# One core, sliding-window attention and expert layers: moving the loads of q, k and v to other places in the queues

## The chip, the cores and the metric

The kernel runs on 1 core of one Trainium2 chip. The metric is the device time of one execution in microseconds (us). Before the change, three runs took 228.25, 230.02 and 230.86; the median is 230.02.

## The reference

For 8 batches, 8 heads, 576 positions and 64 elements a head, each query attends to itself and the 63 positions before it. The result of a batch, 576 x 512, is averaged over its positions; the average picks one of 8 experts, and the batch goes through that expert's two matrices.

```python
scores = scale * np.matmul(q, k.transpose(0, 1, 3, 2))
mask = (rel >= 0) & (rel < window)             # rel = query - key, window = 64
attn = softmax(np.where(mask, scores, -1e9))   # exp, divided by its sum
x = np.matmul(attn, v)                         # heads side by side: B, S, 512
...
logits = x.mean(axis=1) @ w_gate               # 512 -> 8
e_idx = np.argmax(logits, axis=1)
gate_w = softmax(logits)[e_idx]
out = gate_w * (np.maximum(x @ w1[e_idx], 0) @ w2[e_idx])   # 512 -> 1024 -> 512
```

All inputs are float32 in device memory.

## The kernel before

**Units, steps and batches.** The work is cut into 16 units, each half a batch (four heads): unit u belongs to batch u // 2. For a unit, `transpose_qk` turns q and k (TensorE) and ScalarE or VectorE copies them out of PSUM; `scores(u, c)` for c = 0, 1, 2 multiplies q and k, takes the exponential (ScalarE, L389) and, from unit 2 on, multiplies the result tile `pt` with a 0/1 mask (VectorE, L391); `values(u, s)` multiplies `pt` with v (L413) and VectorE divides by the row sums (L427, L429). `cast_part` and `cast_v` make the float16 copies of v that `values` reads (VectorE, L303); `cast_v(u)` does all three parts of a unit. `transpose_x` (L450, L458) prepares the batch's attention result for the expert layers and adds up the gate's input (L476, L480).

**The gate and the experts.** `gate(b)` computes the logits, finds the expert (VectorE, L492 to L500) and loads its number into a register of GpSimd; `load_w1(b)` and `load_w2(b)` then fetch that expert's matrices, 2 MB each in float32, cast to float16 on the way. `expert_up` (L557, eight pieces a batch) and `expert_down` (L571, L580, five pieces) are handed out in small portions by `experts(amount)` between the pieces of attention, so that TensorE always has something to do. The program order written here is the order in which each engine works; each engine takes its instructions strictly in that order.

**The order of the work.** Units 0 to 3 are written out by hand ahead of the loop (L686 to L758); L760 is the loop over steps t = 4 to 19, where step t does the attention of unit t, the transposes of unit t + 1 and expert pieces of earlier batches. `next_gate` (L764) runs gate b = t // 2 - 1 in every even step, so the weights of batch b are fetched in step 2b + 2 and first used in step 2b + 3.

**The loads.** Three kinds of loads matter here.
- `load_qk(u)` (L207) puts two DMAs into GpSimd's queue, q (L211) and k (L214) of one unit, cast to bfloat16. It needs nothing but a free tile; there are six of each.
- `load_w1` and `load_w2` (L534, L539; for batch 0 in two halves, L531) are in GpSimd's queue too, and wait for the gate.
- `load_v(b)` (L220) is a DMA in SyncE's queue (L227), float32, one for a whole batch, three tiles. Ahead of it GpSimd writes one column of the tile; SyncE's DMA waits for that write. Without a second argument the write is a memset (L223), which waits for nothing and holds the DMA only until GpSimd comes to it. With the argument `behind` it is a copy of one column of that tile (L226), so the load starts only when that tile is written.

The output tiles go out through SyncE's queue as well (L575, L588), so output and v stand in one line, in program order.

Before the change the places are these. Ahead of the loop: `load_qk(3)` and `load_qk(4)` after the transposes of unit 1; then gate 0, w1 and w2 of batch 0, `load_qk(5)`, v of batch 2 behind the first half of batch 0's w1, `load_qk(6)`, v of batch 3. In step 4, after gate 1: w1, w2, v of batch 4, `load_qk(7)`. At the head of step 5: `load_qk(8)` and `load_qk(9)`. From then on an even step t has, behind its gate, w1, `load_qk(t + 4)` (up to t = 10), w2, and v of batch t // 2 + 2; an odd step has `load_qk(t + 4)` at its head. q and k are four units ahead.

Of the kernel before, what the change touches and what calls it, by code (L numbers as in the profile page):

```python
# [156 lines left out]
def kernel(  # L157
# [11 lines left out]
    B, H, S, D = q.shape  # L169
# [5 lines left out]
    NU = 2 * B  # L175
# [4 lines left out]
    def P(ins):  # L180
        tc.keep_in_program_order(ins)
        return ins
# [25 lines left out]
    def load_qk(u):  # L208
        qn = qkn.tile([128, 2, NT * D], BF16, tag="qn")
        kn = qkn.tile([128, 2, NT * D], BF16, tag="kn")  # L210
        P(nc.gpsimd.dma_start(out=qn, in_=qv[u]))  # L211
        if u == 0:
            load_v(0)
        P(nc.gpsimd.dma_start(out=kn, in_=kv[u]))  # L214
        qk_tiles[u] = (qn, kn)
# [3 lines left out]
    def load_v(b, behind=None):  # L219
        vn = vpool.tile([128, NM, D], FP32, tag="vn")  # L220
        if behind is None:

            P(nc.gpsimd.memset(vn[:, 0, 0:1], 0.0))  # L223
        else:

            P(nc.gpsimd.tensor_copy(out=vn[:, 0, 0:1], in_=behind))  # L226
        P(nc.sync.dma_start(out=vn, in_=vv[b]))  # L227
        v_tiles[b] = vn
# [70 lines left out]
    def copy_on(eng, out, in_):  # L299
        if eng is nc.scalar:  # L300
            P(nc.scalar.copy(out=out, in_=in_))  # L301
        else:
            P(eng.tensor_copy(out=out, in_=in_))  # L303

    def cast_part(u, part, eng=None):
        b, qd = divmod(u, 2)
        i = b % 2
        vn = v_tiles[b]
        lo, hi = qd * HM, qd * HM + HM
        l1 = max(lo, 1)  # L310

        src = vn if eng is nc.gpsimd else va[i]
        eng = eng or nc.vector
        if part == "whole":
            copy_on(eng, va[i][:, lo:hi, 0:D], vn[:, lo:hi, :])
        elif part == "low":
            copy_on(eng, vb[i][0:64, lo:hi, 0:D], src[0:64, lo:hi, 0:D])
        else:
            copy_on(eng, vb[i][64:128, l1:hi, 0:D], src[64:128, l1 - 1:hi - 1, 0:D])

    def cast_v(u):
        for part in ("whole", "low", "high"):
            cast_part(u, part)

    qt_tiles, kt_tiles, pt_tiles, x_tiles, xt_tiles = {}, {}, {}, {}, {}
# [40 lines left out]
    def scores(u, c):  # L366
        qT, kT = qt_tiles[u], kt_tiles[u]
        masked = (u, c) in sp_ps
        if not masked:
            sp_ps[u, c] = psum.tile([128, 2, 512], FP32, tag="ps", name="sp")  # L370
        sp = sp_ps[u, c]

        def mm(s, half, kblk, qblk, n):
            P(nc.tensor.matmul(  # L374
                out=sp[64 * half:64 * half + 64, s,
                       64 * (qblk - 6 * c):64 * (qblk - 6 * c) + n],
                lhsT=kT[64 * s:64 * s + 64, ts(kblk, 64)],
                rhs=qT[64 * s:64 * s + 64, 64 * qblk:64 * qblk + n],
                start=not masked, stop=not masked or kblk >= g0 + 4,
                tile_position=(64 * s, 64 * half)))  # L380

        g0 = 6 * c
        for s in range(2):
            mm(s, 1, 1 if c == 0 else g0 - 1, g0, 64)
        for g in range(g0, g0 + 6):
            for s in range(2):
                mm(s, g % 2, g, g, 128 if g < g0 + 5 else 64)
        pt = ptp.tile([128, 2, 384], FP16, tag="pt")
        P(nc.scalar.activation(out=pt, in_=sp[:, :, 0:384], func=AF.Exp, scale=scale))  # L389
        if not masked:  # L390
            P(nc.vector.tensor_tensor(  # L391
                out=pt, in0=pt, in1=masks[:, c].rearrange("p s g w -> p s (g w)"),
                op=ALU.mult))
        pt_tiles[u, c] = pt
# [91 lines left out]
    def gate(b):  # L486
        gl = psum.tile([128, 2, 512], FP32, tag="ps", name="gl")
        P(nc.tensor.matmul(out=gl[:, 0, 0:E], lhsT=onesf, rhs=gparts[b],
                           start=True, stop=True))

        glog = small.tile([128, E], FP32, tag="glog")
        P(nc.vector.tensor_copy(out=glog, in_=gl[:, 0, 0:E]))  # L492
        gmx = small.tile([128, 8], FP32, tag="gmx")
        P(nc.vector.max(out=gmx, in_=glog))
        graw = small.tile([128, 8], U32, tag="graw")
        P(nc.vector.max_index(out=graw, in_max=gmx, in_values=glog))
        P(nc.vector.tensor_scalar(out=eidx[:, b, :], in0=graw, scalar1=E - 1,
                                  scalar2=None, op0=ALU.min))
        gnm = small.tile([128, 1], FP32, tag="gnm")
        P(nc.vector.tensor_scalar(out=gnm, in0=gmx[:, 0:1], scalar1=-1.0 / S,  # L500
                                  scalar2=None, op0=ALU.mult))
        gate_in[b] = glog, gnm

        ereg = nc.gpsimd.alloc_register(f"er{b}")
        P(nc.gpsimd.load(ereg, eidx[0:1, b, 0:1]))
        experts_of[b] = ds(nc.gpsimd.snap(ereg, donate=True), 1)
        weights[b] = (wpool.tile([128, KB, F], FP16, tag="w1t", name=f"w1t{b}"),
                      wpool.tile([128, FB, Dm], FP16, tag="w2t", name=f"w2t{b}"))
# [13 lines left out]
    def w1_parts():  # L522
        return weights[0][0].rearrange("p k f -> p (k f)").rearrange(
            "p (h k f) -> p h k f", h=NQ, k=KB)
# [13 lines left out]
    def load_w2(b):  # L538
        P(nc.gpsimd.dma_start(  # L539
            out=weights[b][1].rearrange("p (g i) d -> p g i d", i=4),  # L540
            in_=w2e[experts_of[b]].squeeze(0)))
# [94 lines left out]
    def experts(amount):  # L636

        acc[0] += amount
        while acc[0] > 0.0:
            nxt = next(stream, None)  # L640
            if nxt is None:
                return
            nxt[0]()
            halves[0] = False
            acc[0] -= nxt[1]

            free[0] = nxt[2]

    per_step = (8 * 1.0 + 4 * 1.7 + 0.9) / 2
    START = 3  # L650
# [51 lines left out]
    cast_part(0, "low", nc.gpsimd)  # L702
    load_qk(3)
    load_qk(4)
    cast_part(0, "whole")
    cast_v(1)
    for c in range(3):
# [15 lines left out]
    gate(0)  # L723
    load_w1(0)
    load_w2(0)
    load_qk(5)
    load_v(2, w1_parts()[:, 0, 0, 0:1])
    load_qk(6)
    load_v(3)
    for c in range(3):  # L730
        scores(2, c)
        if c == 0:
# [27 lines left out]
    for t in range(START + 1, NU + LAG):  # L760
        pace = per_step / 8.0 * 0.96
        on, prev, ahead = t < NU, START + 1 < t <= NU, t + 1 < NU

        def next_gate():  # L764
            b = t // 2 - 1
            gate(b)
            load_w1(b)
            if START + 1 < t < NU - 4:
                load_qk(t + 4)
            load_w2(b)  # L770
            if t // 2 + 2 < B:
                load_v(t // 2 + 2)
            if t == START + 1:
                load_qk(7)

        for u in [8, 9] if t == 5 else [t + 4] if t % 2 == 1 else []:
            if u < NU:
                load_qk(u)
        if prev:
            transpose_x(t - 1)  # L780
        if ahead and t > 5:
            cast_part(t + 1, "whole")
        if on:
            scores(t, 0)
            scores(t, 1)
        experts(pace)
        if t == START + 1 or t == NU:
            next_gate()
        if t == NU:
            gate_weight(B - 1)  # L790
            okc = row_check()
        if ahead and t > 5:
            cast_part(t + 1, "low")
            cast_part(t + 1, "high")
        experts(pace)
        if START + 1 < t < NU and t % 2 == 0:
            next_gate()
        if on:
            scores(t, 2)
        if START < t < NU and t % 2 == 0:  # L800
            gate_weight(t // 2 - 1)
        if t == START + 1:
            cast_v(t)
        experts(pace)
        experts(pace)

        if ahead:
            transpose_qk(t + 1, 1, leave=False)
            leave_qk(t + 1, 1, free[0])
        if on:  # L810
            values(t, 0)
        halves[0] = on
        experts(pace)
        experts(pace)
        if ahead:
            transpose_qk(t + 1, 0)
        if on:
            values(t, 1)
        halves[0] = on
        if t in (4, 5):  # L820
            cast_v(t + 1)
        if t == NU:
            row_flag(okc)
        experts(pace)
        experts(pace)
# [38 lines left out]
```

## Time and profile before

| what | value |
|---|---|
| runs | 228.25, 230.02, 230.86 us, median 230.02 |
| the profiled execution, its own time | 230.25 us |
| its span (first to last instruction) | 228.0 us |
| granted TensorE clock, mean | 0.972 |
| GpSimd's DMA queue (q0): packets, MB, share of 16 engines' span | 13840, 26.22, 64.5% |
| SyncE's DMA queue (q1): the same | 15232, 18.88, 27.4% |
| median from issue to landing: w1, w2, v | 8.6, 16.4, 19.9 us |

The profile is one execution. Its rows give a start and a length in us, the engine (PE is TensorE's matmul, DVE is VectorE, ACT is ScalarE, POOL is GpSimd, SP is SyncE), the line of the kernel, the tiles written and read, and in brackets how long the engine had been idle and what ended that idle time. The row of a DMA's issue is the time that the issuing engine spends on it; the time to landing is told apart. A window of the DMA view counts, for each queue, the packets, the MB and the share of the 16 engines' time that its packets took.

### The profile page before, as it was taken

How to read it: one execution, taken by the hardware profiler on the slowest of the kernel's cores; microseconds unless marked ns; L12 is line 12 of the kernel's file. 1: busy time of each engine (PE TensorE's matmuls, PEld its weight loads, DVE VectorE, ACT ScalarE, POOL GpSimd, SP SyncE). 2: the span in 40 equal slices, each digit the busy share in tenths (PEclk: the TensorE clock that was granted, in tenths of full speed). 3: DMA queues.
4: the chain of work that ended last, by engine and by line, in shares of the span. 5: the costliest groups of instructions: out<-in, count | busy, mean ns of one | idle time of the engine just before them, and what ended most of it. 6: DMA issues, size and time to landing. Idle time of an engine off the chain costs nothing.

```text
span 228.0 us, 6994 instructions
## 1 busy us (share of the span) xinstructions
PE 201.8 (88%) x3011; PEld 143.3 (63%) x3012; DVE 130.8 (57%) x309; ACT 133.5 (59%) x219; POOL 40.8 (18%) x69
## 2 busy tenths in 40 slices
PE   7855879997789996999999998999999998999980
PEld 2334668854478473876588556867688557649630
DVE  2629687656747856646674849284948572421130
ACT  2345387783467764694769565877488357416410
POOL 7129063009000070006100430020002000200000
PEclk9979679999999999999999999999999999999997
DMA  5999979999999999998999999999950995399242
GB/s 67 243 256 207 171 110 214 237 254 229 226 230 243 270 232 225 237 244 199 213 241 235 278 197 248 229 299 186 236 168 3 175 225 182 45 218 245 78 145 68
DMA packets 29910, 45.64 MB, mean 200 GB/s; under 512 B 2480, under 2 KB 21936, under 8 KB 29872
## 3 DMA queue, kind: packets, MB, share of 16 engines
q0 software_dynamic: 13840, 26.22, 64.5%
q1 hardware_dynamic: 15232, 18.88, 27.4%
q8 instruction: 25, 0.41, 0.7%
q10 hardware_dynamic: 800, 0.03, 0.2%
q14 instruction: 13, 0.11, 0.1%
HBM read 61.90 MB, written 9.44 MB: 313 GB/s over the span
## 4 chain that ended last, share of the span: by engine, by line
PE 57%; DMA 16%; ACT 12%; DVE 8%; issue 2%; POOL 1%; POOLq 0%
PE php L557 23%; PE pso L571 19%; DMA w1t<-in_moe_w_dram 11%; PE tp L334 6%; DMA kn<-in_k_dram 4%; ACT xT L458 4%; ACT pt L389 4%; PE op L413 4%; ACT hT L561 4%; PE pso L580 2%; DVE x L429 1%; PE sp L374 1%; DVE va L303 1%; PE tp L450 1%; DVE vb L303 1%
## 5 line engine op out<-in xcount | busy, mean ns | idle before, releaser
L557 PE MATMUL php<-xT,w1t 128*128 128x288 f16 x512 | 69.8, 287 | 4.7 <-DMA w1t<-in_moe_w_dram 4.1
L561 ACT ACTIVATE hT<-php,gatew 128x576 f16<-128x576 f32 x64 | 46.9, 746 | 31.3 <-PE php L557 31.3
L557 PEld LDWEIGHTS <-w1t 128*128 128x128 f16 x512 | 55.6, 114 | 12.0 <-DMA w1t<-in_moe_w_dram 5.3
L571 PE MATMUL pso<-w2t,hT 128*128 128x512 f16 x256 | 60.5, 380 | 1.0 <-ACT hT L561 0.9
L389 ACT ACTIVATE pt<-sp 128x768 f16<-128x768 f32 x48 | 36.6, 821 | 9.8 <-PE sp L374 9.8
L571 PEld LDWEIGHTS <-hT 128*128 128x128 f16 x256 | 23.3, 98 | 27.7 <-issue 1.8
L303 DVE COPY ob<-pso 128x512 f32<-128x512 f32 x24 | 16.5, 689 | 24.2 <-PE pso L571 24.1
L534 POOL DMA_DIRECT2D w1t<-in_moe_w_dram x7 | 5.0, 716 | 138.1 <-PE tp L334 63.0
L391 DVE TENSOR_TENSOR pt<-pt,masks 128x768 f16<-128x768 f16 x42 | 23.3, 555 | 8.0 <-ACT pt L389 6.7
L429 DVE TENSOR_TENSOR x<-op,linv 128x640 f16<-128x640 f32 x32 | 26.4, 824 | 1.1
L347 ACT COPY dst<-tp 128x1152 bf16<-128x1152 bf16 x16 | 17.9, 1119 | 15.3 <-PE tp L334 15.1
L458 ACT ACTIVATE xT<-tp 128x576 f16<-128x576 f16 x28 | 17.9, 647 | 6.2 <-PE tp L450 6.2
L413 PE MATMUL op<-vb,pt 128*64 128x65 f16 x320 | 16.0, 195 | 5.1 <-DVE vb L303 1.5
L413 PEld LDWEIGHTS <-pt 128*64 128x64 f16 x640 | 13.7, 111 | 7.3 <-issue 3.7
L303 DVE COPY dst<-tp 128x1152 bf16<-128x1152 bf16 x9 | 12.2, 1355 | 7.3 <-PE tp L334 7.2
L374 PE MATMUL sp<-dst 64*64 64x128 bf16 (+1 forms) x672 | 14.1, 218 | 2.3 <-ACT dst L301 1.0
L480 DVE SCALAR_TENSOR_TENSOR gpart<-wg,pooled,gpart 128x8 f32<-128x8 f32 x21 | 4.8, 226 | 19.3 <-ACT xT L458 19.2
L413 PE MATMUL op<-va,pt 128*64 128x65 f16 x320 | 15.7, 195 | 0.0
L374 PEld LDWEIGHTS <-dst 64*64 64x64 bf16 x672 | 10.6, 110 | 7.5 <-issue 2.5
L427 DVE RECIPROCAL linv<-op 128x10 f32<-128x10 f32 x32 | 6.9, 217 | 14.0 <-PE op L413 13.8
L303 DVE COPY vb<-va 64x1152 f16<-64x1152 f16 (+1 forms) x30 | 14.2, 475 | 0.4
L303 DVE CAST va<-vn 128x1152 f16<-128x1152 f32 x16 | 13.8, 865 | 0.5 <-DMA vn<-in_v_dram 0.5
(72 smaller groups left out, 183.1 us busy)
## 6 DMA issues: line engine op xcount, KB each, us to landing
w2t<-in_moe_w_dram POOLq DMA_DIRECT2D x8, 1024.0 KB, 16.4
out_dram<-ob SPq DMA_DIRECT2D x32, 256.0 KB, 7.5
w1t<-in_moe_w_dram POOLq DMA_DIRECT2D x7, 1024.0 KB, 8.6
qn<-in_q_dram POOLq DMA_DIRECT2D x16, 288.0 KB, 12.5
kn<-in_k_dram POOLq DMA_DIRECT2D x16, 288.0 KB, 14.2
w1t<-in_moe_w_dram POOLq DMA_DIRECT2D x2, 512.0 KB, 6.4
out_dram<-ob SPq DMA_DIRECT2D x16, 64.0 KB, 7.5
vn<-in_v_dram SPq DMA_DIRECT2D x8, 0.2 KB, 19.9
```

Of the source, the lines that this page charges most:

```text
L303: P(eng.tensor_copy(out=out, in_=in_))
L334: P(nc.tensor.transpose(out=tp[64 * s:64 * s + 64, ts(t, 128)], in_=src[:, s, ts(t, D)], identity=ident, tile_position=(0, 64 * s)))
L347: P(nc.scalar.copy(out=dst.rearrange("p (x r t) -> p x r t", x=2, t=NT), in_=view))
L374: P(nc.tensor.matmul(out=sp[64 * half:64 * half + 64, s, 64 * (qblk - 6 * c):64 * (qblk - 6 * c) + n], lhsT=kT[64 * s:64 * s + 64, ts(kblk ...
L389: P(nc.scalar.activation(out=pt, in_=sp[:, :, 0:384], func=AF.Exp, scale=scale))
L391: P(nc.vector.tensor_tensor(out=pt, in0=pt, in1=masks[:, c].rearrange("p s g w -> p s (g w)"), op=ALU.mult))
L413: P(nc.tensor.matmul(out=op[64 * half:64 * half + 64, xx, 65 * jj:65 * jj + 65], lhsT=pt[:, s, 64 * (g % 6):64 * (g % 6) + 64], rhs=win, s ...
L429: P(nc.vector.tensor_tensor(out=x[:, :, h0 * D:(h0 + 2) * D].rearrange("p j (x c) -> p x j c", x=2), in0=view[:, :, :, 0:64], in1=li[:, :, ...
L458: P(nc.scalar.activation(out=xT[:, kb, :], in_=tp[:, kl, 0:S], func=AF.Copy, accum_out=pooled[:, b, kb:kb + 1]))
L557: P(nc.tensor.matmul(out=php[:, sc, 0:288], lhsT=w1t[:, kb, cols], rhs=xT[:, kb, ts(sc, 288)], start=(kb == 0), stop=(kb == KB - 1)))
L561: P(nc.scalar.activation(out=hT[:, ft].rearrange("p (sc s) -> p sc s", sc=2), in_=php[:, :, 0:288], func=AF.Relu, scale=gatew[:, b:b + 1]))
L571: P(nc.tensor.matmul(out=pso[:, 0, :], lhsT=hT[:, fb, ts(mt, 128)], rhs=w2t[:, fb, :], start=(fb == 0), stop=(fb == FB - 1)))
```

## The change

Six loads or groups of loads get other places; no computation is changed.

- `load_qk(5)` moves ahead of the first gate, right behind `load_qk(4)`.
- v of batch 3 moves from ahead of the loop into step 4, behind `scores(4, 2)`, and is tied to that score tile, written last by its mask; `load_qk(7)` follows it.
- v of batches 4 to 7 moves from the even steps' gates to the odd steps t = 5, 7, 9, 11, after the first two score tiles, and is tied to the first of them.
- q and k are three units ahead: `load_qk(t + 3)` between w1 and w2 in even steps 6 to 12, and in odd steps up to 11 ahead of v.

```diff
     load_qk(3)
     load_qk(4)
+    load_qk(5)
     cast_part(0, "whole")
...
     load_w1(0)
     load_w2(0)
-    load_qk(5)
     load_v(2, w1_parts()[:, 0, 0, 0:1])
     load_qk(6)
-    load_v(3)
...
             gate(b)
             load_w1(b)
-            if START + 1 < t < NU - 4:
-                load_qk(t + 4)
+            if START + 1 < t < NU - 3:
+                load_qk(t + 3)
             load_w2(b)
-            if t // 2 + 2 < B:
-                load_v(t // 2 + 2)
-            if t == START + 1:
-                load_qk(7)
-
-        for u in [8, 9] if t == 5 else [t + 4] if t % 2 == 1 else []:
-            if u < NU:
-                load_qk(u)
+
         if prev:
             transpose_x(t - 1)
...
         if on:
             scores(t, 0)
             scores(t, 1)
+        if t % 2 == 1:
+            if t + 3 < NU:
+                load_qk(t + 3)
+            if (t + 3) // 2 < B:
+
+                load_v((t + 3) // 2, pt_tiles[t, 0][:, 0, 0:1])
         experts(pace)
...
         if on:
             scores(t, 2)
+        if t == START + 1:
+            load_v(3, pt_tiles[t, 2][:, 0, 0:1])
+            load_qk(7)
         if START < t < NU and t % 2 == 0:
```

## The prediction

> **What bounds the kernel now.** I read the page's busy line and slices first, then the chain of waits, then TensorE's and VectorE's timelines where the chain names a DMA, and last the packets of the two DMA queues in short windows. Times are us from the start of the profiled span. w1(b), w2(b), v(b) and q/k(u) are the loads of batch b and unit u; step t works on unit t.
>
> ```profile
> PE 201.8 (88%) x3011; PEld 143.3 (63%) x3012; DVE 130.8 (57%) x309; ACT 133.5 (59%) x219; POOL 40.8 (18%) x69
> DMA  5999979999999999998999999999950995399242
> ```
> ```profile
> 28.89 5.26 DMA w1t<-in_moe_w_dram
> ...
> 51.13 12.11 DMA w1t<-in_moe_w_dram
> ...
> 80.58 8.61 DMA w1t<-in_moe_w_dram
> ```
> ```profile
> 63.29 1.17 PE L557 MATMUL php<-xT,w1t 128*128 128x288 f16 x8 [1.85 <-DMA w1t<-in_moe_w_dram]
> ...
> 89.23 1.17 PE L557 MATMUL php<-xT,w1t 128*128 128x288 f16 x8 [2.26 <-DMA w1t<-in_moe_w_dram]
> ```
>
> TensorE is busy 88% and the DMA engines are full for three quarters of the span, yet what DMA costs is little: the chain runs through w1(0), whose first half lands at 28.89 + 5.26 = 34.15 and starts the expert matmuls, and TensorE waits 1.85 for w1(1) and 2.26 for w1(2). VectorE waits once for v(2), below. All else that the reordering could win is under transfers that nobody waits for. So the ceiling of the gain is 1.85 + 2.26 + 0.49 = 4.6 us, and the question is what the new places of the loads make late.
>
> How two queues share the engines sets every landing time. q0 is GpSimd's (weights, q, k), q1 is SyncE's (v, output). Pairs of rows of the DMA view, for 90:92 (q/k beside v), 96:98 (a weight beside v), 86:88 (a weight, v just starting), 54:55 (v alone) and 55:56:
>
> ```profile
> q0 software_dynamic: 232, 0.25, 73.0%
> q1 hardware_dynamic: 231, 0.24, 42.6%
> ...
> q0 software_dynamic: 91, 0.37, 89.9%
> q1 hardware_dynamic: 92, 0.09, 16.9%
> ...
> q0 software_dynamic: 112, 0.40, 100.5%
> q1 hardware_dynamic: 7, 0.01, 1.2%
> ...
> q1 hardware_dynamic: 216, 0.22, 113.3%
> ...
> q0 software_dynamic: 15, 0.06, 30.2%
> ```
>
> The queues take turns packet by packet. A q, a k or a weight is 256 packets (128 rows in two pieces), a v is 1,152 of 1 KB (1.18 MB). So v moves 115 packets a us beside q/k, 45 beside a weight, 215 alone; a weight moves 56 a us alone and 45 beside v. Landings, in us from issue, of v(2), v(5), w1(3), w1(5), w1(6):
>
> ```profile
> vn<-in_v_dram SPq DMA_DIRECT2D x1, 0.2 KB, 17.4
> ...
> vn<-in_v_dram SPq DMA_DIRECT2D x1, 0.2 KB, 20.1
> ...
> w1t<-in_moe_w_dram POOLq DMA_DIRECT2D x1, 1024.0 KB, 8.3
> ...
> w1t<-in_moe_w_dram POOLq DMA_DIRECT2D x1, 1024.0 KB, 9.8
> ...
> w1t<-in_moe_w_dram POOLq DMA_DIRECT2D x1, 1024.0 KB, 8.9
> ```
>
> **The change, part by part.**
>
> *q/k(5) ahead of the first gate.* Two more DMA issues on GpSimd, some 0.7 each, where it would otherwise wait for gate 0; they cost it nothing. Their 512 packets run behind k(4)'s. q0 in 23:24, 27:28, 28:29, 30:31:
>
> ```profile
> q0 software_dynamic: 186, 0.20, 122.3%
> ...
> q0 software_dynamic: 158, 0.17, 99.8%
> q0 software_dynamic: 32, 0.03, 17.7%
> ...
> q0 software_dynamic: 11, 0.01, 42.5%
> ```
>
> At the mean of the first two (172 a us) 512 packets take 3.0 us. k(4) ends near 28.2, w1(0) begins near 30.9: a hole of 2.7 takes most of them, and w1(0) is late by 0.3. The ends are 0 and 3.0 (no hole used). TensorE has no cover there: **+0.3**. Behind w1(0) stand w2(0), q/k(6) and v(2). v(2) loses the company of 512 q/k packets and moves as many alone: 512 / 115 - 512 / 215 = 2.1 sooner, less the 0.3.
>
> ```profile
> 51.21 0.56 DVE L391 TENSOR_TENSOR pt<-pt,masks 128x768 f16<-128x768 f16 x1 [0.43 <-ACT pt L389]
> ...
> 52.34 0.81 DVE L303 CAST va<-vn 128x1152 f16<-128x1152 f32 x1 [0.49 <-DMA vn<-in_v_dram]
> 53.18 1.22 DVE L303 COPY vb<-va 64x1152 f16<-64x1152 f16 x2
> ...
> 71.84 0.75 DVE L303 CAST va<-vn 128x1152 f16<-128x1152 f32 x1
> ...
> 74.33 0.23 DVE L480 SCALAR_TENSOR_TENSOR gpart<-wg,pooled,gpart 128x8 f32<-128x8 f32 x1 [0.78 <-ACT xT L458]
> 74.96 0.23 DVE L480 SCALAR_TENSOR_TENSOR gpart<-wg,pooled,gpart 128x8 f32<-128x8 f32 x1 [0.41 <-ACT xT L458]
> ```
>
> v(2) landed at 52.3 and would now at 50.5. That ends VectorE's wait at 52.34: **-0.5**; more than 0.49 can't be had there.
>
> *w1(1).* It was issued at 51.13, yet its first packets show in 55:56; until 55 the engines carried only v. In the same time VectorE cast v(2) from 52.34 to 54.40, and a GpSimd memset, else 0.12, took 0.63:
>
> ```profile
> 52.55 0.63 POOL L223 MEMSET vn<- 128x1 f32 x1
> ...
> 83.43 0.12 POOL L223 MEMSET vn<- 128x1 f32 x1
> ```
>
> So either v crowded it out, or the cast kept GpSimd from writing its descriptors. The Trainium skill's SBUF — State Buffer (SBUF: two separate sides) says the second: a VectorE copy in a two-port mode locks GpSimd out of the shared port, and a DMA of GpSimd's waits for its descriptors. By that rule the casts, now right behind the mask, hold w1(1) as before; without it, w1(1) gains about 2 us here. No row here separates them. The memset is the row nearest to the question, so I take the hold: first packet near 55.7, landing 63.0 against 63.24, **-0.2**. The other end is a first packet at 53.5, landing near 60, and the whole wait of TensorE (free at 61.43) gone: -2.
>
> *v(3) behind unit 4's third mask.* The mask ends at 51.77, and GpSimd comes to the copy only after w2(1), where the memset of 52.55 stood, so the tie itself waits for nothing; the place in GpSimd's order is what moves v(3), from right behind q/k(6) to about 53.1, when the first cast lets the copy through. Behind it on GpSimd stand q/k(7) and (8), not urgent; on SyncE, batch 0's output. v(5), issued at 83.64 (row below), had 7 packets through at 88: 4.2 to the first. So the first at 57.3; by then w1(1) has moved 1.6 x 56 = 90. 166 packets go beside the rest of it and 256 beside w2(1) (422 / 45 = 9.4), 730 beside q/k(7) and (8) (730 / 115 = 6.3), together 73.0. v(5), counted so (4.2 + 256 / 45 + 896 / 115 = 17.7), landed at 20.1, 2.4 later, of which some 0.5 went beside the end of w1(2); with 1.9, v(3) lands near 74.9. The ends are 17.4 and 22 after issue (70.5, 75.1; 22 is this working). VectorE cast it at 71.84, now 71.6: a **new wait of 3.3 us** for v(3), with the units' masks, the output copies and gate 2 queued behind it. From the start of that cast to the issue of w1(2) are 80.58 - 71.84 = 8.74, of which 0.78 + 0.41 are idle, so 7.55 when VectorE is late: issue at 82.45 against 80.58.
>
> *w1(2) and output.* q0 is empty now when w1(2) is issued, but so far output was held behind v:
>
> ```profile
> 83.64 0.77 SPq L227 DMA_DIRECT2D vn<-in_v_dram  x1
> 84.50 13.46 SPq L575 DMA_DIRECT2D out_dram<-ob  x1
> ```
>
> With v tied to odd steps, output goes out in the even step, beside the weight. w1(3), alone, took 8.3; w1(5) and w1(6), beside output, 9.8 and 8.9. I take 8.9: landing 91.35 against 89.19, **+2.1**, which contains the terms above, since this chain hangs on v(3) alone. Ends 8.3 and 9.8: +1.5 and +3.0; with v(3) at 70.5, -2.3 (rival 2).
>
> *Steps 9 and 11.* The expert matmul of step 9 comes 113.47 - 104.77 = 8.7 after w1(3)'s issue; step 11 is alike:
>
> ```profile
> 104.77 0.72 POOL L534 DMA_DIRECT2D w1t<-in_moe_w_dram  x1 [19.87 <-PE tp L334]
> ```
> ```profile
> 113.47 2.15 PE L557 MATMUL php<-xT,w1t 128*128 128x288 f16 x16
> ```
>
> At 8.9 each waits 0.2: **+0.4** (ends 0 and 2.2).
>
> *Later v, q and k.* At nothing. v(7) is the tightest: issued at about 138.5 behind unit 11's mask, 20.1 later 158.6, cast at 159.79:
>
> ```profile
> 137.10 1.15 DVE L391 TENSOR_TENSOR pt<-pt,masks 128x768 f16<-128x768 f16 x2
> ...
> 159.79 0.76 DVE L303 CAST va<-vn 128x1152 f16<-128x1152 f32 x1
> ```
>
> If it took 22, VectorE would wait 0.7. v(4) follows v(3) at about 72 and is alone from 77; it lands near 84, before its cast at 86 and more. q and k have two steps, 24.2 us (89.23 to 113.47), and landed in 14 at the median.
>
> Sum: 2.1 + 0.4 = +2.5 on the profiled execution's 230.25 (span 228.0). That execution is 0.2 above the median, 230.02, so **232.5** against the median.
>
> **The rivals.** (1) *v(3) a little sooner, no loss* (against the forecast's sign). If w1(1) is not held by the casts, it has 256 - 3.8 x 56 = 43 packets left beside v(3) instead of 166: v(3) lands 123 / 45 - 123 / 115 = 1.7 sooner, at 73.2, and w1(2) at 73.2 + 7.55 + 8.6 = 89.35, with the 8.61 that it took before. That is +0.2, and 0.2 at step 9: 230.4. It decides from v(3) landing before 73.5. For it: the engines were full of v in 54:55, and v(2) would be out of the way. Against: the memset. (2) *v(3) in time.* At v(2)'s 17.4 it lands at 70.5; with w1(1) not held either, step 5 starts 2.0 sooner, VectorE's idle covers the rest, and w1(2) comes at 80.58 - 2.0 + 8.3 = 86.9: -2.3, 227.7. Against: v(2) ran beside one weight, v(3) does beside nearly two. (3) *The wait at step 7 halves TensorE's clock.* TensorE reached that matmul at 89.23 - 2.26 = 86.97; with the masks of step 6 late by up to 1.5 it would be idle some 3 us before 91.35. Windows 11.40:17.10, 85.50:91.20:
>
> ```profile
> 11.40:17.10 5.70, 3.41 (x42) 2.19 (x42) 1.50 (x2) 2.54 (x4) 1.25 (x3) 0.71 1.16 256
> ...
> 85.50:91.20 5.70, 3.44 (x34) 2.08 (x33) 3.56 (x8) 2.75 (x6) 0.00 (x0) 1.00 1.09 224
> ```
>
> With the same busy time one stretch lost clock (0.71) and the other, with 2.26 of idle, none. A loss of that size, 0.29 of 5.7, is 1.65: 232.5 + 1.65 = 234.2. The Trainium skill's TensorE: Matmul & The Clock Gate (Part 1, What's actually happening) halves the clock after an idle window of about 3.4 us; here 2.26 did not trip it, and by that rule 3 would only where a window falls just so.
>
> **How the numbers follow.** The forecast has 0.42, with 231.3 to 233.5 as its own range; rival 1 0.30; rival 2 0.12; rival 3 0.16. About 1% (2.3 us, 232.3) is what a measurement can tell from no change. Slower: rival 3 whole, 0.24 of the forecast's 0.42, and some of rival 1's late ends, together 0.44. Faster (below 227.7): half of rival 2 and the chance that later waits of TensorE shrink unseen, 0.10. Within: 0.46. The range leaves out the better part of rival 2 and the worst of rival 3, some 0.15: 228.0 to 235.0.
>
> **What would show it.** Right: VectorE's cast of v(3), near 72, waits 3 us for its DMA; w1(2) is issued after 82; TensorE waits longer than 2.26 before step 7's first expert matmul, and about as long as before at step 5. Wrong: no wait at that cast (rival 2); w1(1)'s first packets within 2.5 us of its issue and TensorE not waiting at step 5 (rival 1); a granted clock below 1 near 91 (rival 3); waits for v in later steps, which I costed at nothing.

## The result, and the profile after

The changed kernel takes **242.81 us** at the median (four runs, 241.05 to 243.99), against 229.77 for the kernel before on the same chip (four runs): a ratio of **1.0557, interval 1.0496 to 1.0619**. Slower, as forecast, but five times as much as the 2.5 us that the forecast's sum gave, and above its range. In this and all later comparisons the ratio leaves out disturbed runs and the median does not, so the two need not agree to the last tenth.

The page of the changed kernel, in the order in which the page before was read: the busy line, and the 40 slices of the granted clock and of the DMA engines.

```profile
PE 209.3 (86%) x3011; PEld 144.9 (60%) x3012; DVE 129.1 (53%) x309; ACT 133.3 (55%) x219; POOL 41.9 (17%) x69
...
PEclk9979988999999796799979999799999999999997
DMA  6999999919999999993999879996996499199331
```

TensorE runs as many matmuls as before, but is busy 209.3 us instead of 201.8: 7.5 more, for the same work. The clock's slices say why: behind the first load phase there are four dips, at slices 14 (a 7), 16 and 17 (6 and 7), 21 and 26 (7 each), where the kernel before, whose row is here, has none.

```profile
PEclk9979679999999999999999999999999999999997
```

Next, as before, the chain of waits of the changed kernel, and TensorE's timeline at the first expert matmuls of batches 0 to 4 (steps 3, 5, 7, 9, 11; in brackets how long TensorE had been idle, and for what):

```profile
54.99 20.86 DMA vn<-in_v_dram
75.94 0.77 DVE va L303
...
83.33 10.44 DMA w1t<-in_moe_w_dram
...
111.79 10.62 DMA w1t<-in_moe_w_dram
...
139.06 12.02 DMA w1t<-in_moe_w_dram
```
```profile
34.40 3.82 PE L557 MATMUL php<-xT,w1t 128*128 128x288 f16 x16 [2.54 <-DMA w1t<-in_moe_w_dram]
...
63.05 1.14 PE L557 MATMUL php<-xT,w1t 128*128 128x288 f16 x8 [0.67 <-DVE ob L303]
...
93.82 2.11 PE L557 MATMUL php<-xT,w1t 128*128 128x288 f16 x8 [3.95 <-DMA w1t<-in_moe_w_dram]
...
122.45 3.23 PE L557 MATMUL php<-xT,w1t 128*128 128x288 f16 x16 [1.89 <-DMA w1t<-in_moe_w_dram]
...
151.13 2.11 PE L557 MATMUL php<-xT,w1t 128*128 128x288 f16 x8 [3.29 <-DMA w1t<-in_moe_w_dram]
```

Read the brackets and the lengths together. The wait for w1(1) is gone (0.67, on VectorE), but there are waits for w1(0), w1(2), w1(3) and w1(4), and behind each of them the matmuls are slow: 16 take 3.82 or 3.23 where they took 2.15, eight take 2.11 where they took 1.17. The windows of the changed kernel around those places (fields: busy time and count of PE, PEld, DVE, ACT and POOL, then granted clock, DMA share, GB/s) give the clock:

```profile
34.00:38.00 4.00, 3.60 (x16) 2.24 (x16) 0.43 (x1) 0.74 (x1) 1.62 (x3) 0.57 1.15 211
79.00:83.00 4.00, 4.00 (x33) 1.53 (x28) 3.70 (x13) 1.55 (x4) 0.00 (x0) 0.58 1.07 229
92.00:100.00 8.00, 6.18 (x70) 4.04 (x71) 1.39 (x3) 2.19 (x3) 0.00 (x0) 0.57 1.11 232
123.00:127.00 4.00, 4.00 (x52) 2.89 (x49) 0.58 (x2) 1.49 (x2) 0.00 (x0) 0.57 1.16 244
150.00:154.00 4.00, 2.87 (x24) 1.86 (x26) 0.77 (x2) 0.73 (x1) 0.00 (x0) 0.58 1.15 250
```

A mean of 0.57 over 4 us is half clock for 3.4 us; over 8 us it is two such stretches. TensorE does 1.7 us less work in each stretch. Six stretches make 10.2; the kernel before loses two of them at 24.08 to 30.91 (its slices 5 and 6), where the changed kernel loses none, so that about the 7.5 above is left. The stretch from 79 follows no weight but VectorE, late with the cast of 75.94. The Trainium skill's TensorE: Matmul & The Clock Gate (Part 1, What's actually happening) has a window of about 3.4 us, and these stretches agree with that length.

Three rows of the kernel before are needed to see where the 14.1 us of span (242.1 against 228.0) come in: the issue of its w1(4), what that load took, and the first expert matmul of step 11.

```profile
128.67 0.72 POOL L534 DMA_DIRECT2D w1t<-in_moe_w_dram  x1 [19.58 <-PE tp L334]
...
137.37 1.17 PE L557 MATMUL php<-xT,w1t 128*128 128x288 f16 x8
```
```profile
w1t<-in_moe_w_dram POOLq DMA_DIRECT2D x1, 1024.0 KB, 8.2
```

| stretch | before | after | more | forecast |
|---|---|---|---|---|
| start to step 5's first expert matmul | 63.29 | 63.05 | -0.24 | -0.2 |
| from there to the issue of w1(2) | 17.29 | 20.28 | +2.99 | +2.1 |
| issue of w1(2) to step 7's first expert matmul | 8.65 | 10.49 | +1.84 | +0.3 |
| from there to the issue of w1(3) | 15.54 | 17.97 | +2.43 | 0 |
| issue of w1(3) to step 9's | 8.70 | 10.66 | +1.96 | +0.2 |
| from there to the issue of w1(4) | 15.20 | 16.61 | +1.41 | 0 |
| issue of w1(4) to step 11's | 8.70 | 12.07 | +3.37 | +0.2 |

These add up to 13.76. Three kinds of rows make it: the way over v(3) to w1(2)'s issue (3.0, about as forecast), the landing times of w1(2) to w1(4) (7.2 against 0.7 forecast), and the matmuls behind each wait, slow by the clock (3.8 against nothing).

Why do these weights land late? Two rows of SyncE's timeline of the changed kernel (a pair of output tiles, and v(6)), and its packets in 84:85 and 85:86 (behind w1(2)'s issue at 83.33), 113:114 and 119:120 (behind w1(3)'s at 111.79):

```profile
113.41 2.40 SPq L588 DMA_DIRECT2D out_dram<-ob  x2
...
121.51 0.77 SPq L227 DMA_DIRECT2D vn<-in_v_dram  x1
```
```profile
q1 hardware_dynamic: 142, 0.26, 68.5%
...
q0 software_dynamic: 21, 0.09, 95.4%
q1 hardware_dynamic: 14, 0.02, 8.7%
...
q1 hardware_dynamic: 119, 0.21, 72.3%
q0 software_dynamic: 4, 0.02, 11.8%
...
q0 software_dynamic: 35, 0.14, 89.1%
q1 hardware_dynamic: 34, 0.03, 11.4%
```

In 84:85 only q1 has a row; each other window has two. In the first microseconds behind a weight's issue the engines carry output (q1). Near its end q1 runs beside the weight again and takes a packet for each of the weight's. That is output too, and not yet the odd step's v: v's first packets come at 95.69, 125.79 and 153.26, behind the landings of all three weights (93.77, 122.41, 151.08). In the kernel before it is v that runs at that place, and the output is held behind it. What q1 moves from 6 us behind a weight's issue to its landing, and in the first 2 us, in MB:

| | w1(2) | w1(3) | w1(4) |
|---|---|---|---|
| from 6 us to the landing, before (v) | 0.12 | 0.09 | 0.06 |
| the same, after (output) | 0.36 | 0.32 | 0.50 |
| first 2 us, before | 0.38 | 0.12 | 0.48 |
| the same, after | 0.30 | 0.25 | 0.25 |

So a burst of output at the issue is nothing new, though for w1(3) it has doubled; the output beside the later part of the weight is. Whether it is what makes the weight late, and whether the slow clock is a cause or only company, the experiments had to tell.

### The profile page after: what moved, and what is told of

The parts are those of the page before. It is cut to its first block, busy times and chain, and to the rows that moved or that the text cites. A ratio compares the mean times of both kernels' runs of the same rounds, so it can differ in the third digit from the quotient of the medians.

```text
span 242.1 us, 6997 instructions
## 1 busy us (share of the span) xinstructions
PE 209.3 (86%) x3011; PEld 144.9 (60%) x3012; DVE 129.1 (53%) x309; ACT 133.3 (55%) x219; POOL 41.9 (17%) x69
## 4 chain that ended last, share of the span: by engine, by line
PE 49%; DMA 29%; ACT 9%; DVE 6%; issue 2%; POOL 1%; POOLq 0%; DVEq 0%; SPq 0%
PE php L557 22%; DMA w1t<-in_moe_w_dram 17%; PE pso L571 15%; DMA vn<-in_v_dram 9%; PE tp L334 5%; DMA kn<-in_k_dram 4%; ACT xT L458 3%; ACT hT L561 3%; PE op L413 3%; ACT pt L389 3%; PE pso L580 2%; DVE x L429 1%; DVE vb L303 1%; DVE va L303 1%; PE sp L374 1%
## 5 line engine op out<-in xcount | busy, mean ns | idle before, releaser
L557 PE MATMUL php<-xT,w1t 128*128 128x288 f16 x512 | 75.3, 302 | 12.9 <-DMA w1t<-in_moe_w_dram 11.7
L557 PEld LDWEIGHTS <-w1t 128*128 128x128 f16 x512 | 57.2, 117 | 23.3 <-DMA w1t<-in_moe_w_dram 13.0
L571 PE MATMUL pso<-w2t,hT 128*128 128x512 f16 x256 | 62.2, 388 | 1.0 <-ACT hT L561 0.9
L389 ACT ACTIVATE pt<-sp 128x768 f16<-128x768 f32 x48 | 36.6, 821 | 10.9 <-PE sp L374 10.9
L347 ACT COPY dst<-tp 128x1152 bf16<-128x1152 bf16 x16 | 18.0, 1123 | 13.5 <-PE tp L334 13.2
L374 PE MATMUL sp<-dst 64*64 64x128 bf16 (+1 forms) x672 | 14.1, 216 | 2.5 <-ACT dst L301 1.2
L374 PEld LDWEIGHTS <-dst 64*64 64x64 bf16 x672 | 10.5, 109 | 8.1 <-issue 2.8
L303 DVE CAST va<-vn 128x1152 f16<-128x1152 f32 x16 | 12.5, 787 | 4.3 <-DMA vn<-in_v_dram 4.3
L334 PE MATMUL tp<-ident,kn 128*64 128x128 bf16 x288 | 12.9, 244 | 1.6 <-DMA kn<-in_k_dram 1.6
```

What stands on the lines that cost most here:

```text
L334: P(nc.tensor.transpose(out=tp[64 * s:64 * s + 64, ts(t, 128)], in_=src[:, s, ts(t, D)], identity=ident, tile_position=(0, 64 * s)))
L347: P(nc.scalar.copy(out=dst.rearrange("p (x r t) -> p x r t", x=2, t=NT), in_=view))
L374: P(nc.tensor.matmul(out=sp[64 * half:64 * half + 64, s, 64 * (qblk - 6 * c):64 * (qblk - 6 * c) + n], lhsT=kT[64 * s:64 * s + 64, ts(kblk ...
L557: P(nc.tensor.matmul(out=php[:, sc, 0:288], lhsT=w1t[:, kb, cols], rhs=xT[:, kb, ts(sc, 288)], start=(kb == 0), stop=(kb == KB - 1)))
L571: P(nc.tensor.matmul(out=pso[:, 0, :], lhsT=hT[:, fb, ts(mt, 128)], rhs=w2t[:, fb, :], start=(fb == 0), stop=(fb == FB - 1)))
```

## Experiments

**Theory O**: v tied to the odd steps lets output out in even steps, beside the weights, and that makes w1(2) to w1(4) late; TensorE then waits, its clock halves, and each step passes its delay on. **Rival V**: it is v at the tail of each weight. **Rival Q**: q and k, three units ahead, crowd the weights. Beside them stand the loads ahead of the loop: q/k(5) and v(3).

### The later v

*The changed kernel with v(5) to v(7) back behind the gates* (v(4) stays at step 5's mask).

```diff
             load_w2(b)
+            if START + 1 < t and t // 2 + 2 < B:
+                load_v(t // 2 + 2)
...
-            if (t + 3) // 2 < B:
-                load_v((t + 3) // 2, pt_tiles[t, 0][:, 0, 0:1])
+            if t == 5:
+                load_v(4, pt_tiles[t, 0][:, 0, 0:1])
```

> v of batches 5 to 7 is loaded at the gates of steps 6, 8 and 10 again, as before the change; all else is as after it. Theory O (with v in the odd steps SyncE's queue is free in the even steps, so output is sent beside w1 and makes it late, and the clock halves in the wait): output is held behind v again, w1 of steps 6, 8 and 10 lands in about 8.3 to 8.6 us instead of 10.4, 10.6 and 12.0, TensorE waits for it under 1 us in all at steps 9 and 11, and no clock is lost after 100; 231 to 234 us. Rival S (w1 is late because of q and k being three units ahead, or the queue order around the gate): w1 stays at 10 us and more, the clock still halves at steps 9 and 11, 240 us and more.

Measured: 232.44 (231.07 to 233.72), ratio 1.0085, 1.0023 to 1.0147. The waits for w1 of the changed kernel, and of this one (us in all, how many, the longest):

```profile
PE php L557 <- DMA w1t<-in_moe_w_dram: 11.7, 4, 4.0
```
```profile
PE php L557 <- DMA w1t<-in_moe_w_dram: 4.5, 2, 2.5
```

Most of the loss (some 11 of 13 us) is gone with one part of the change: w1(2) to w1(4) land in 8.1 to 8.3, nothing waits at steps 9 and 11, and behind 42 us the clock stays whole. The two waits left are those for w1(0) (2.50) and w1(2) (1.97).

*The kernel before with that part alone*: v(5) to v(7) in steps 7, 9 and 11, all else as it was.

```diff
-            if t // 2 + 2 < B:
+            if t == START + 1:
                 load_v(t // 2 + 2)
...
+        if t in (7, 9, 11):
+            load_v((t + 3) // 2, pt_tiles[t, 0][:, 0, 0:1])
         experts(pace)
```

> As before the change, with only v of batches 5 to 7 moved to the odd steps 7, 9 and 11 and tied to their first masked tile; q/k(5), v(3), v(4) and the four units of lead are as before. If this part alone makes w1 late: w1 of steps 8 and 10 takes 9.5 to 12 us instead of 8.3 and 8.2, TensorE waits at steps 9 and 11, 233 to 238 us. If it needs the late v(3) or the shorter lead of q and k: within 1 us of before, 229 to 231.

Measured: 237.0 (234.63 to 241.0), ratio 1.026, 1.0187 to 1.0333. TensorE waits 3.22, 2.18 and 3.60 at steps 7, 9 and 11; the weights land in 9.6, 10.9 and 12.1, and clock is lost twice. The part costs 6 to 7 us by itself, without any late v(3): so the late weights don't need the other parts, but together they cost more than apart (13 us, against 6.5 here and 1.8 in the run above).

### Output or v

*The changed kernel with no output sent from steps 6 to 11* (so it leaves out those output tiles, and nothing else).

```diff
-            P(nc.sync.dma_start(out=out[b, ts(mt, 128), :], in_=ob))
+            send(lambda: P(nc.sync.dma_start(out=out[b, ts(mt, 128), :], in_=ob)))
...
+        drop[0] = 6 <= t <= 11
```

> As after the change, but the output DMAs that steps 6 to 11 issue are left out (most of the outputs of batches 1 to 3 are not written); v stays in the odd steps. Theory O, now with the finding that output held behind v comes out as a burst when v is nearly done: w1 of steps 6, 8 and 10 lands in 8.0 to 8.5 us, no wait over 1 us at steps 9 and 11, 231 to 235 us. Rival V (v's own tail in the odd step is enough): w1 of steps 8 and 10 still takes 9.5 us and more, 236 us and more.

Measured: 233.3 (231.5 to 234.77), ratio 1.013, 1.007 to 1.0191. Its waits for w1, and the landing of its w1(3):

```profile
PE php L562 <- DMA w1t<-in_moe_w_dram: 4.3, 2, 2.4
```
```profile
w1t<-in_moe_w_dram POOLq DMA_DIRECT2D x1, 1024.0 KB, 7.8
```

v stands in the odd steps as in the changed kernel, and yet the weights land in 8.0, 7.8 and 7.9 and steps 9 and 11 don't wait. So output makes the weights late. Rival Q is out, since q and k stand as in the changed kernel. Rival V this run doesn't test, since here too v's first packets come behind the landings (the nearest is v(5), 94.84 against 91.17). It falls by the packets above: no v runs beside the three late weights, and in the kernel before, where v does run at their end, they land in 8.2 to 8.6.

*The changed kernel with the output of steps 6 to 11 held back* until the odd step's v is issued: the order that SyncE had before, made by hand.

```diff
             load_w2(b)
+            hold[0] = START + 1 < t < 12
...
                 load_v((t + 3) // 2, pt_tiles[t, 0][:, 0, 0:1])
+            hold[0] = False
+            while held:
+                held.pop(0)()
```

> As after the change, with the output DMAs of steps 6 to 11 issued from behind each gate until the odd step's v load kept back and sent right after that load; v stays in the odd steps. Theory O: w1 of steps 6, 8 and 10 has the engines to itself, lands in 8.0 to 8.6 us, TensorE's waits at steps 9 and 11 go, 231 to 235 us. Rival V (v's own place in the odd step is what hurts, by its tail beside the next w1 or by its late landing): the waits stay, 240 us and more.

Measured: 235.87 (234.24 to 237.67), ratio 1.0237, 1.0164 to 1.0309. More than half of the loss is gone, not all. w1(2) lands in 8.0, but w1(3) and w1(4) take 9.5 and 10.3. SyncE's timeline of this kernel, and its packets in 107:108, behind w1(3)'s issue at 106.72:

```profile
91.83 12.92 SPq L582 DMA_DIRECT2D out_dram<-ob  x1
104.84 1.18 SPq L596 DMA_DIRECT2D out_dram<-ob  x2
106.11 1.02 SPq L582 DMA_DIRECT2D out_dram<-ob  x2
```
```profile
q1 hardware_dynamic: 195, 0.31, 83.9%
```

v, now late in the odd step, holds SyncE's queue for 12.92 until 104.84, just ahead of the next gate, and the output held behind it comes out right beside the next weight. In the kernel before, v behind the gate held output from 84.50 for 13.46, to 97.96: the output came in the middle of the odd step, behind one weight and 6.8 ahead of the issue of the next (104.77). This fits O: with its output held, w1(2) is no longer late, and the two weights that the held burst meets still are. That burst is larger than any in the table above: 0.58 and 0.68 MB in the first 2 us behind the issue.

### The clock

*The changed kernel with twelve idle matmuls ahead of the first expert matmul of batches 2 to 4*, so that TensorE works while it waits.

```diff
+        if ft == 0 and 2 <= b <= 4:
+            busy(12)
         if ft == 0:
```

> As after the change, with 12 idle matmuls (2.6 us of work on nothing) ahead of the first expert matmul of batches 2, 3 and 4, where TensorE waits for w1. If the clock halves because TensorE stands idle there: it stays at 1.0 from 85 on, the first matmuls of these steps take their 287 ns, and the time falls by 3 to 6 us, to 237 to 240; the w1 latencies stay at 10 to 12. If the clock halves for another reason, or costs nothing because the next w1 is late anyway: the time stays within 1 us, or grows.

Measured: 238.58 (235.62 to 240.58), ratio 1.0282, 1.0203 to 1.036. The weights are as late as in the changed kernel (10.3, 10.5, 10.9), but these windows of this kernel show what its clock did around its steps 7, 9 and 11:

```profile
90.00:98.00 8.00, 7.03 (x126) 5.95 (x127) 3.18 (x6) 4.18 (x6) 0.00 (x0) 1.00 1.12 232
118.00:122.00 4.00, 4.00 (x64) 3.53 (x63) 1.51 (x3) 1.48 (x2) 0.00 (x0) 1.00 1.15 238
140.00:150.00 10.00, 10.00 (x139) 6.96 (x138) 7.04 (x14) 5.66 (x9) 0.51 (x1) 1.00 1.10 232
```

So TensorE's idleness behind a late weight is what halves the clock, and that is worth some 4 us of the 13 by the medians. Part of that may be chance: in the profiled run the clock is whole at w1(0) and behind VectorE's late cast of v(3) as well, where no idle matmul stands. The weights' lateness and the waits that it makes remain.

### The loads ahead of the loop

*The changed kernel with v(3) back behind q/k(6)*, ahead of the loop.

```diff
     load_qk(6)
+    load_v(3)
...
-            load_v(3, pt_tiles[t, 2][:, 0, 0:1])
             load_qk(7)
```

> v of batch 3 is loaded ahead of the loop again, behind q and k of unit 6; all else is as after the change. If the 4.3 us wait of VectorE's cast for v(3) costs what the chain says: the wait is gone, gate 2 issues w1 about 2.5 us sooner, the halved clock near 79 to 82 is gone, but w1 of batch 1 is late again by about 1.8 us; steps 9 and 11 still wait, so 239 to 241 us. If the waits at steps 7, 9 and 11 descend from the late v(3) (everything behind it shifted against the loads), they go too: 232 us or less.

Measured: 233.98 (230.75 to 237.56), ratio 1.003, 0.9966 to 1.0094. The runs spread by 7 us, so the total decides little. The rows of the profiled one (231.56):

```profile
PE php L557 <- DMA w1t<-in_moe_w_dram: 8.9, 5, 2.8
```
```profile
113.00:118.00 5.00, 4.39 (x65) 3.91 (x66) 3.69 (x8) 1.93 (x4) 0.22 (x1) 1.00 1.17 256
138.00:146.00 8.00, 5.81 (x106) 5.05 (x107) 5.19 (x10) 3.38 (x5) 0.26 (x1) 1.00 1.11 245
```

Its w1(3) and w1(4) are still late (9.7 and 11.5) and TensorE waits 8.9 us in all, the longest 2.79, yet the clock is whole in both windows. With these two weights nearly as late as in the changed kernel and no lost clock, the time is nearly that of before. The four runs point the same way: 231.56 and 230.75 had a mean granted clock of 0.981 and 0.973, 236.4 and 237.56 one of 0.958 and 0.955. This says again how much of the loss is the clock, and that whether a wait of 2 to 3 us trips it changes from case to case.

*The changed kernel with q/k(5) back behind w2(0).*

```diff
     load_qk(4)
-    load_qk(5)
...
     load_w2(0)
+    load_qk(5)
```

> q and k of unit 5 stand behind w2 of batch 0 again; all else is as after the change. If q/k(5) delays w1 of batch 0 and that wait halves the clock: TensorE waits under 0.5 us for w1(0), the clock stays 1.0 from 34 to 38, and the time falls by 1.5 to 2 us, to about 241. If the halving near 35 comes from the 1.2 us wait ahead of it anyway: same clock, same time within 0.5 us.

Measured: 239.64 (235.96 to 240.58), ratio 1.0315, 1.0215 to 1.0415: some 3 us better than the changed kernel by the medians. TensorE waits 0.26 for w1(0) instead of 2.54, and the 16 matmuls behind it take 2.15 instead of 3.82. The wait for w1(2) stays (4.23).

*The kernel before with v(3) alone moved behind unit 4's third mask* (and v(4), which must follow it, to step 5's mask).

```diff
     load_qk(6)
-    load_v(3)
...
+        if t == 5:
+            load_v(4, pt_tiles[t, 0][:, 0, 0:1])
         experts(pace)
...
             scores(t, 2)
+        if t == START + 1:
+            load_v(3, pt_tiles[t, 2][:, 0, 0:1])
```

> Before, with v(3) moved behind unit 4's third mask and v(4), which must follow it, to step 5's mask; q/k(5), all other q, k and v as before. By the prediction VectorE waits 3 to 4 us for v(3) near 72 to 76 and w1(2) is issued 2 us later, so that with w1(2) in 8.6 the time is 231.5 to 232.5. By its rival w1(1), free of v, lands in 8.5 and gives that back at step 5: 229 to 230.5. If the clock halves in a wait before step 7, 234.

Measured: 233.26 (231.1 to 234.7), ratio 1.0103, 1.004 to 1.0166. In the profiled run, the slowest of the four, VectorE's cast waits 3.92 for v(3), w1(1) lands in 8.5, and TensorE waits 4.51 for w1(2). The part costs 1%, 2.4 us: near what the forecast's sum gave for the whole change, but in the profiled run not by its terms. There w1(2) is issued at 80.58, the same as in the kernel before, and lands in 10.6, with v(4) on the engines at its issue; the loss is in that landing and in the half clock behind the wait (3.4 us from 91.37).

*v(3) tied to unit 4's first mask instead of its third*, an attempt to have it in time; q/k(5) and v(5) to v(7) are at their old places, v(4) at step 5's mask, q and k three ahead.

```diff
             scores(t, 1)
+        if t == START + 1:
+            load_v(3, pt_tiles[t, 0][:, 0, 0:1])
         if t % 2 == 1:
...
             scores(t, 2)
-            load_v(3, pt_tiles[t, 2][:, 0, 0:1])
```

> A version put together from the parts: q/k(5) and v of batches 5 to 7 at their old places, v(3) in step 4 but ahead of gate 1, tied to unit 4's first masked tile (some 6 us sooner than in the change), v(4) in step 5 and q and k three units ahead as changed. If the theories hold: w1 of batch 1 lands 9 to 10 us after issue instead of 12.1 (a gain of 1 to 1.8 at step 5), v(3) lands before its cast (no wait over 0.5), w1 of step 6 takes 8.1 instead of 8.6, w1 of steps 8 and 10 about 8.2 and no clock is lost: 227 to 229 us. If v(3) beside w1(1) costs as much as v(4) did: 230, no difference to before.

Measured: 231.52 (229.95 to 234.38), ratio 1.0032, 0.9981 to 1.0083: no difference, and the gain hoped for isn't there. v(3) is in time, but w1(1), issued at 50.67, now takes 13.2 and TensorE waits 3.39 for it.

*The changed kernel with q/k(5), v(3) and v(5) to v(7) all at their old places* (q/k(5) and the gates as in the diffs above), so that only v(4) and the three units' distance of q and k are left of the change.

```diff
     load_qk(6)
+    load_v(3)
...
             scores(t, 2)
-            load_v(3, pt_tiles[t, 2][:, 0, 0:1])
...
-            if (t + 3) // 2 < B:
-                load_v((t + 3) // 2, pt_tiles[t, 0][:, 0, 0:1])
+            if t == 5:
+                load_v(4, pt_tiles[t, 0][:, 0, 0:1])
```

> q/k(5) and v(3) stand where they stood before, v(5) to v(7) at the gates; of the change only v(4) at step 5's mask and q and k three units ahead remain. If the loss is made of its three parts (q/k(5) at the head, v(3) late, output beside the later weights) and nothing else, this lands within 1% of before, 228 to 231, with w1(2) to w1(4) in 8 to 9 us and no wait of TensorE over 1 us at steps 9 and 11. If the new places of q, k and v(4) cost something by themselves, 233 or more, with a late w1(2) or a wait for q or k.

Measured: 230.08 (227.91 to 232.52), ratio 0.9992, 0.9951 to 1.0032. The rest of the change costs nothing, as forecast.

*The kernel before with q/k(5) alone moved ahead of gate 0.*

```diff
     load_qk(4)
+    load_qk(5)
...
     load_w2(0)
-    load_qk(5)
```

> Before, with nothing changed but q/k(5) queued ahead of gate 0. By the prediction's term the first expert matmul comes 0.3 later and the time stays at 230 to 230.5. By what the changed kernel showed, TensorE waits over 2 us for w1(0) and then runs its first matmuls at half clock: first batch of 16 in 3.8 to 4.0 instead of 2.15, some 1.5 to 2 us, and the time is 231.5 to 233, unless v(2) landing sooner gives part of it back at step 5.

Measured: 231.75 (228.88 to 233.52), ratio 1.0034, 0.9989 to 1.0078. Here two effects meet. TensorE's timeline of this kernel at w1(0), then its packets in 53:54, 54:55 and 55:56, around w1(1)'s issue at 53.94, and VectorE's cast of v(2):

```profile
35.33 3.82 PE L557 MATMUL php<-xT,w1t 128*128 128x288 f16 x16 [2.48 <-DMA w1t<-in_moe_w_dram]
```
```profile
q1 hardware_dynamic: 192, 0.19, 97.9%
...
q1 hardware_dynamic: 27, 0.02, 8.9%
...
q0 software_dynamic: 15, 0.06, 89.0%
```
```profile
54.57 0.74 DVE L303 CAST va<-vn 128x1152 f16<-128x1152 f32 x1
55.34 1.15 DVE L303 COPY vb<-va 64x1152 f16<-64x1152 f16 x2
```

At the head it loses 2.5 us of wait and 1.67 of clock, and w1(1) is issued 2.81 later than in the kernel before. At step 5 it wins 1.9 of that back (the first expert matmul comes at 64.20 against 63.29): v(3) has run out when w1(1) is issued, and w1(1) lands in 8.3 instead of 12.1, although the casts lie in the first microseconds behind its issue.

*The same, with eight idle matmuls ahead of the first expert matmul of batch 0*, to keep the gain and not the lost clock.

```diff
+        if ft == 0 and b == 0:
+            busy(8)
         if ft == 0:
```

> Before with q/k(5) ahead of gate 0, as in the run with that part alone, and with eight idle matmuls on TensorE ahead of the first expert matmul, so that it isn't idle while it waits for w1(0). If idleness is what halves the clock behind that wait, the first 16 expert matmuls take 2.15 again instead of 3.82, and, with w1(1) still landing in 8.3, the time is 228.5 to 229.5, up to 0.6% below before. If the clock falls all the same, or the idle matmuls push the expert matmuls back by as much as they save, 230.5 to 231.5 as without them.

Measured: **228.92** (227.22 to 232.34) against 229.97, ratio **0.996, 0.9923 to 0.9997**. The same place in this kernel's timeline, and its clock from 33 to 37:

```profile
32.16 1.90 PE L658 MATMUL idle<-spin 128*128 128x512 bf16 x7
34.08 2.15 PE L559 MATMUL php<-xT,w1t 128*128 128x288 f16 x16
```
```profile
33.00:37.00 4.00, 3.92 (x44) 2.80 (x44) 1.88 (x6) 2.69 (x4) 1.73 (x4) 1.00 1.20 208
```
With the clock whole, q/k(5) ahead of the gate is the one part of the change that pays, by 0.4%; the interval ends just short of no difference. It is the only kernel here whose interval lies below 1, and the gain is small. Idle matmuls without q/k(5) weren't tried; at its old place TensorE's wait for w1(0) is 0.26 to 0.73 in the runs here, so there is little to fill.

## Why the prediction was right or wrong

- *The bound* was read rightly: what w1 makes TensorE wait decides, and nothing else of the change (q and k three ahead, v(4)) costs anything: ratio 0.9992 with those alone.
- *q/k(5) ahead of the first gate*: **wrong in size**. I took the hole in the engines' time as nearly big enough and put the wait at 0.3, with 3.0 as the far end. TensorE waits 2.54 (0.26 with q/k(5) back), and the matmuls behind it lose 1.67 more to the clock. The hole of 2.7 stood in an execution with a late gate 0 (w1(0) issued at 28.89); in the changed kernel w1(0) is issued at 27.19, while q/k(5) runs until 31.15, and takes 7.16 instead of 5.26. I had asked that question about step 7 only, not about the first wait. Undone, it gave 3 us.
- *w1(1)*: **the mechanism that I chose was the wrong one.** I let VectorE's casts hold the weight, by the memset of 0.63 and the rule of the Trainium skill's SBUF — State Buffer (SBUF: two separate sides). In the changed kernel w1(1) landed in 8.5, and with q/k(5) alone moved in 8.3, with the casts 0.6 behind its issue. What had made 12.1 of it was v(3), which was streaming when it was issued: with v(3) tied to step 4's first mask it was streaming again, and w1(1) took 13.2. So rival 1's condition held, but not what it made of it: v(3) landed at 75.85 and not before 73.5. The 3.6 us that w1(1) gained were mostly eaten at the head, and step 5 came 0.24 sooner, close to the 0.2 forecast, by errors that cancel and by luck: gate 0 issued w1(0) 1.70 sooner in this execution than in the kernel before's. Over all fourteen profiles that issue lies at 27.19 to 28.20 with q/k(5) ahead of the gate and at 26.95 to 28.89 without, so it isn't the change that moved it.
- *v(3) behind unit 4's third mask*: **right**. The cast waits 4.28 (forecast 3.3), and from the cast's start to w1(2)'s issue are 7.4 us (forecast 7.55). Here is the row:

```profile
75.94 0.76 DVE L303 CAST va<-vn 128x1152 f16<-128x1152 f32 x1 [4.28 <-DMA vn<-in_v_dram]
```

- *w1(2) and output*, with *steps 9 and 11*: **this is the step that failed.** That output would go beside the weight was seen; its price was taken as 8.9 from w1(5) and w1(6) of the kernel before, with 9.8 as the worst. Those two met less of it: from 6 us behind the issue to the landing q1 moved 0.26 MB beside w1(5) and 0.10 beside w1(6), against the 0.36, 0.32 and 0.50 here. Measured: 10.4, 10.6 and 12.0, and 7.8 to 8.0 with that output left out. Steps 9 and 11, costed at 0.4 in all with 2.2 as the far end, lost 5.3 in the weights' landing alone.
- *Rival 3, the clock*: it had 0.16 for one place, and came true in four places behind the first load phase (three behind a late weight, one behind VectorE's late cast) and once at the head. The bound that I took from 2.26 us of idle without a loss was no bound: 1.89 lost clock at step 9. And I added no rival's price to another's, though late weight and slow clock go together: the wait makes the slow clock, and the slow matmuls make the next gate late.
- *The range* failed for that reason: its top held one lost stretch and one late weight, and the change had three late weights and six lost stretches.
- *Parts and whole*: alone, v in odd steps costs 2.6%, v(3) 1.0%, q/k(5) 0.3%, 4.0% in all (the parts are rounded); together they cost 5.6%. The four intervals together leave about 1.2 points of doubt on the 1.6 between, so that it is only just clear of noise, and where it comes from isn't taken apart by these runs.

## What to carry to other kernels

A queue's order is also a timetable for what stands behind the moved item: before moving a load, list what its wait has been holding back, and look where that will run instead; here v's place kept each batch's output away from the weights. Where one wait of the busiest engine appears in every round of a loop, cost it in every round, and add the clock that it loses to the wait itself. And a gain that a lost clock eats can be had by giving the engine idle work in that wait: that made the one useful part of this change visible.

## What the runs showed of the hardware

- **Waits of about 2 us are a toss-up for the clock.** Waits of TensorE for w1 of 3.2 us or more (3.22, 3.29, 3.39, 3.60, 3.95, 4.23, 4.51) went with half clock. Of shorter ones some did (1.89, 2.17, 2.42, 2.48, 2.50, 2.54) and some did not (2.11, 2.18, 2.25, 2.26, 2.79). The stretch at half clock lasted 3.41 us or twice that. Much of the toss-up is where the wait falls. In each of the fourteen traces all changes of the clock lie a multiple of 3.413 us apart (in the changed kernel 34.60, 38.01, 78.97, 82.39, 92.63, 99.45, 123.35, 126.76, 150.65, 154.07), so the stretches between stand on a fixed grid. Where TensorE was busy for less than 0.42 of such a stretch at full clock, half clock followed every time; between 0.42 and 0.68 it did in some, and above in none. The wait of 1.89 lay whole in one stretch (119.93 to 123.35, busy 1.53 of 3.42, 0.45); the one of 2.79 was cut by an edge into two (135.48 to 138.89 and on to 142.31, busy 1.92 and 2.12 of 3.41). What decides between 0.42 and 0.68 stays open. The Trainium skill's TensorE: Matmul & The Clock Gate (Part 1, What's actually happening) slows the clock after an idle window of about 3.4 us, which 1.89 and 2.5 do not fill, so the measurement goes beyond it; that the window runs freely, as it says, agrees with the grid.
- **A weight issued while v streams alone does not share at first.** In the kernel before, w1(1) was issued at 51.13, and in 53:54 the engines carried v only, with the weight's first packets in 55:56:

```profile
q1 hardware_dynamic: 213, 0.22, 110.6%
```

  Once both queues run they alternate packet by packet (35 of the weight and 34 of output in the rows of 119:120 above). When v had run out before the issue, or did so within the first microsecond, the weight's first packets came 1 to 2 us behind it. Output did not hold a weight off so: the weight of 83.33 had its first packet 1.84 behind its issue, with 142 of output in 84:85, and w1(4) of the kernel before 1.45, with 0.48 MB of output in its first 2 us, against 1.47 for w1(3) of the kernel that sends no output in steps 6 to 11.
